# Weight conversion and weight product moved eight units earlier, reloaded weights split at a lower rate

## The chip, the cores and the metric

The kernel runs on one core of a Trainium2 chip. The metric is the device time of one execution in microseconds (us); of the kernel before there are three runs with a median of 712.68 us (711.45 to 714.77). The engines are named as the profile names them: PE is TensorE (PEld its weight loads), DVE is VectorE, ACT is ScalarE, POOL is GpSimd, and SP is the engine that issues nearly all DMAs, in order.

## The reference

Three layers follow one another. The first is attention over 2 x 8 heads, 768 rows and 64 columns per head, where a row sees only keys of the same hash bucket (six bits, the signs of a small projection). The second takes the attention's output x (1536 x 512) and multiplies it with four weights. The third routes each row to one of eight experts.

```python
h = (x @ w1) * (x @ w2) @ w3          # w1, w2: 512 x 1024, w3: 1024 x 1024
y = h @ w_out                         # w_out: 1024 x 512
e = argmax(y @ w_gate + modality_bias[modality_id])
out[mask] = gate_w[mask, None] * (relu(y[mask] @ e_w1[e]) @ e_w2[e])   # per expert e
```

The weights w1, w2, w3 and w_out arrive as 64-bit floats. In the kernel every operand of the second and third layer is split in a high and a low part, and each product is made of three matmuls (high-high, high-low, low-high).

## The kernel before, in words

**Units.** The attention part is one loop over i (L719). Unit i has a first stage (L312): two matmuls make the scores `m` of 128 query rows of one head, and DVE takes their row maximum (L324). There are 96 such units: pair of heads i // 12, and in it row block and head. The second stage (L345) follows nine units later: four matmuls make transposed scores `s`, ACT takes the exponential `pt` (L353), POOL adds it up in `acc` (L359; one in six on DVE near the end). Two units later still, two times two matmuls multiply `pt` with v (`a`, L367). Every six units PE transposes the row maxima (`f`, L335), for which four small POOL instructions (L328 to L331) have to be done first, and every twelve units it sums `acc` (`n`, L383).

**Weights.** Beside this the loop converts the weights, in 40 pieces of 128 x 512. A piece is loaded by SP into a ring of three buffers `cr` (L439), three DVE instructions turn its 64-bit patterns into 32-bit floats (L484, L485, L474), and then a piece of w_out or w3 is split: ACT copies the high part (L465), POOL subtracts (L466). A piece of w1 or w2 is written to a DRAM tensor `wfd` instead (L480), since there is no room for it yet. How many pieces are begun by the end of unit i is a ramp through points (unit, pieces), `RAMP` (L36): none by unit 7, 10 by unit 19, all by unit 84. The DVE instructions of a piece are popped from a list at three places of each unit (`fill`, L489).

**The product.** w3 times w_out is folded to one matrix: 8 x 8 x 3 = 192 matmuls of 128 x 128 by 512 (L544), `W34_STEP` = 3.1 per unit, taken from a list in `w34_step` (L556) as soon as both halves of the w3 row block are split. Each eighth is evacuated, written to DRAM and multiplied with the gate weights by three small PE steps in the units behind it (`wt` L519, `pg` L527, `pt` L535).

**Reload.** At unit `SWITCH` = 86 the buffers of the conversion are given back (L721), the tiles `w12` for w1 and w2 take their room, and the 16 pieces of `wfd` are loaded (`st`, L442) and split: ACT copies (L465), DVE subtracts (L466). They are begun at `RATE2` = 1.4 per unit, counted from unit 87 on (L844). At units 90 to 95 the first 256 rows of the attention's output are normalised (`norm_step`, L589): two DVE instructions (L581, L583) with one of POOL between them (L582), an ACT copy (L585) and a DVE subtraction (L587). From unit 95 to 104 a unit has no `m` any more, or one last, and takes twelve matmuls of the next layer (L618) in its place.

**What sets the order.** All of this is one list per engine, written in the order of the Python code; each engine runs its own list in order and waits where an operand or buffer isn't ready. So an instruction that waits holds up everything behind it on its engine.

Of the kernel before, what the change touches and what calls it, by code (L numbers as in the profile page):

```python
# [21 lines left out]
HP = H // 2  # L22
# [10 lines left out]
NCH = NT // CH  # L33

PRE = 0
RAMP = ((7, 0), (19, 10), (84, 41))  # L36
RATE2 = 1.4
W34_STEP = 3.1
SWITCH = 86
LEAD = 9  # L40
NDVE = 0
ACC_DVE = ((76, ()), (96, (2,)))
# [12 lines left out]
NSTEP = 4  # L55
# [36 lines left out]
def pieces_at(i):  # L92
    for (a, x), (b, y) in zip(RAMP, RAMP[1:]):
        if i < b:
            return int(x + (y - x) * max(i - a, 0) / (b - a))
    return RAMP[-1][1]

# [59 lines left out]
def body(tc, qT, kT, vP, w1d, w2d, w3d, wod, mod, wgate, mbias, e1, e2, cst, out):  # L157
# [30 lines left out]
    def ps(tag, shape, name):  # L188
        return psum[0].tile(shape, F32, tag=tag, name=name, bufs=nbuf.get(tag, 1))
# [220 lines left out]
    r_wo = ring("wo", 2 * 8 * DM, 1)  # L410
    wo = r_wo([P, 2, 8, DM], F32R)
    w3_t, raws, w12 = {}, {}, {}
    order = list(range(8))
    w3i, w12i = list(range(8, 24)), list(range(24, 40))
    while w3i or w12i:
        for k in PATTERN:
            src = w3i if k else w12i
# [3 lines left out]
    done = {"n": 0, "w": 0, "q": 0}  # L421
    dq, misc = [], []

    def piece_load(k):
        i = order[k]
        if k in raws:
            return
        if i < 8:
            src = wod[i * P:(i + 1) * P, :]
        elif i < 24:  # L430
            f, hf = divmod(i - 8, 2)
            src = w3d[f, :, hf * 4:hf * 4 + 4, :].rearrange("p g f -> p (g f)")
        else:
            m, j = divmod((i - 24) % 16, 8)
            c, hf = divmod(j, 2)
            src = ((w1d, w2d)[m] if i < 40 else wfd[m])[c * P:(c + 1) * P, hf * 512:hf * 512 + 512]
        if i < 40:
            raws[k] = r_cr([P, 1024])
            SP.dma_start(raws[k].bitcast(I64), src)  # L439
        else:  # L440
            raws[k] = r_st([P, 512])
            SP.dma_start(raws[k], src)  # L442
# [64 lines left out]
    w34q = []  # L507
# [5 lines left out]
    def after(n, fn):  # L513
        todo_at.setdefault(slot[0] + n, []).append(fn)

    def w34_t(f, ev):
        t = ps("m", [P, 4, P], f"wt{f}")
        for c in range(4):
            PE.transpose(t[:, c, :], ev[:, c * P:c * P + P], ident)  # L519
        wT = r_wT([P, 4, P])  # L520
        ACT.copy(wT, t)
        after(1, lambda: w34_gate(f, wT))
# [17 lines left out]
    def w34_mm(f, g, k):  # L540
        if g == 0 and k == 0:
            w34p[f] = ps("w", [P, DM], f"w{f}")
        st, mv = ((0, 0), (0, 1), (1, 0))[k]
        PE.matmul(w34p[f], w3_t[f][:, st, g, :], wo[:, mv, g, :], start=(g == 0 and k == 0), stop=(g == 7 and k == 2))  # L544
        if g == 7 and k == 2:
            ev = r_ev([P, DM])
            ACT.copy(ev, w34p.pop(f))
            SP.dma_start(w34d[f * P:(f + 1) * P, :], ev)
            after(1, lambda: w34_t(f, ev))

    for f in range(8):
        for g in range(8):
            for k in range(3):
                w34q.append((f, lambda f=f, g=g, k=k: w34_mm(f, g, k)))

    def w34_step(n):  # L556
        while n and done["w"] < len(w34q) and order.index(9 + 2 * w34q[done["w"]][0]) < done["n"]:
            w34q[done["w"]][1]()
            done["w"] += 1
            n -= 1  # L560
            if done["w"] % 24 == 0:
                break
# [26 lines left out]
    def norm_step(ch, step):  # L589
        for hp, part in ((step - 2, 2), (step - 1, 1), (step, 0)):  # L590
            if 0 <= hp < HP:
                norm_x(ch, hp, part)
# [126 lines left out]
    for i in range(NU + LEAD + LAG + 2):  # L719
        slot[0] = i  # L720
        if i == SWITCH:  # L721
            assert done["n"] == 40 and done["w"] == len(w34q), done
            for r in (r_cr, r_T, r_ev, r_wT, r_w3, r_wo):
                r.close()
            w12 = [one(f"w{m}", [P, 2, 4, DF], F32R) for m in range(2)]
            r_st = ring("st", 512, 3)
            for m in (40, 41, 42):
                piece_load(m)
            for r in (r_raw, r_bt, r_lo):
                r.close()  # L730
            rg["x"] = ring("x", 2 * HP * CH, 1, True)
            rg["rb"] = ring("rb", HP * CH, 1, True)
            rg["nw"] = ring("nw", CH, 1, True)
            rg["gf"] = ring("gf", 4 * CH, 1, True)
            rg["asb"] = ring("asb", CH, 1, True)
# [9 lines left out]
        if i == 12:  # L745
            SP.dma_start(cs[:, 160:], cst[:, 160:])
            SP.dma_start(wgs[:, :, 0:E], wgate.rearrange("(c p) e -> p c e", p=P))
        if i == SWITCH + NSTEP - 2:
            load_r(0)
        if 0 <= i - SWITCH - NSTEP < HP + 2:  # L750
            norm_step(0, i - SWITCH - NSTEP)
        if i == 98:
            load_r(1)
        if 101 <= i < 101 + HP:
# [22 lines left out]
        for fn in todo_at.pop(i, []):  # L777
            fn()
        w34_step(int((i + 1) * W34_STEP) - int(i * W34_STEP) if i < SWITCH - 1 else 1000)
        j = i - LEAD  # L780
# [10 lines left out]
        n = j - LAG - 1  # L791
# [46 lines left out]
        flush()  # L838
        if i < SWITCH - 1:
            want_pieces(min(40, pieces_at(i)))  # L840
        elif i < SWITCH + 2:
            want_pieces(40)
        else:
            want_pieces(min(56, 40 + int((i - SWITCH - 1) * RATE2)))  # L844
        if i == SWITCH - 1 or i >= NU + LEAD:
# [87 lines left out]
    for ch in range(NCH):  # L933
        if ch:
            g_t[ch] = rg["g"]([P, 2, 8, CH], F32R)
        for f in range(NEARLY if ch == 0 else 0, 8):
            if ch == 0:
                k = f - NEARLY
# [508 lines left out]
```

## Time and profile before

| | |
|---|---|
| median of three runs | 712.68 us |
| the profiled execution's own time | 713.29 us |
| its span, first to last instruction | 711.5 us |
| busy share: PE, DVE, ACT, POOL | 94%, 54%, 44%, 45% |
| attention part, until the last `m` | 0 to 300.5 us |
| mean granted clock of PE | 0.974 |

The profile is of one execution. Busy time of an engine is the time in which an instruction of it runs; a matmul's end is modelled, so where PE is busy all the time the step from start to start says more than the length. In a timeline several instructions of one kind that follow one another stand in one row with their count. The granted clock is a share of full speed: 1.0 is 2.4 GHz, 0.5 is 1.2 GHz. The chain of work that ended last is of no use here: the profile could follow it back for under a microsecond.

### The profile page before, as it was taken

What the parts mean: (1) busy time and instruction counts of PE and PEld (TensorE: products, weight loads), DVE (VectorE), ACT (ScalarE), POOL (GpSimd) and SP (SyncE); (2) the same over time, 40 slices, a digit from 0 to 9 for tenths busy, and PEclk for the clock granted to TensorE, in tenths of its full rate; (3) what the DMA queues carried; (4) which work ended last, traced back from release to release, by engine and by line L of the source; (5) the groups of instructions that cost most, each with busy time, mean ns of one, the idle gap of its engine ahead of it and who ended that gap; (6) DMA issues with size and microseconds to landing.
All of it is one profiled execution on the core that took longest, in us unless ns stands there. A gap on an engine that the chain in (4) does not pass through costs nothing. (4 is left out here: it accounts for less than half of the span.)

```text
span 711.5 us, 11037 instructions
## 1 busy us (share of the span) xinstructions
PE 666.1 (94%) x4004; PEld 506.4 (71%) x4004; DVE 382.2 (54%) x611; ACT 315.1 (44%) x534; POOL 320.6 (45%) x316
## 2 busy tenths in 40 slices
PE   5988999989998999799999999999998999999994
PEld 1444655656555655366999999898987999899983
DVE  6787675746576664857361212121175765665550
ACT  7255554535546554454341313131213765565551
POOL 8489767677767667555260505050214132011110
PEclk9599999999999999899999999999999999999998
DMA  7746545273645634230312020200017786766630
GB/s 226 238 169 171 199 136 182 78 210 103 194 140 144 198 99 128 88 120 1 107 48 60 2 59 1 60 1 30 1 53 270 269 286 232 235 207 210 209 119 5
DMA packets 42122, 94.06 MB, mean 132 GB/s; under 512 B 6784, under 2 KB 12464, under 8 KB 42064
## 3 DMA queue, kind: packets, MB, share of 16 engines
q1 hardware_dynamic: 39984, 86.76, 38.7%
q0 software_dynamic: 2080, 6.56, 2.7%
q8 instruction: 33, 0.54, 0.3%
q14 instruction: 25, 0.20, 0.1%
HBM read 72.98 MB, written 12.98 MB: 121 GB/s over the span
## 5 line engine op out<-in xcount | busy, mean ns | idle before, releaser
L618 PEld LDWEIGHTS ab<-x,w 128*128 128x128 f32 x1152 | 139.9, 191 | 10.5 <-issue 4.8
L618 PE MATMUL ab<-x,w 128*128 128x256 f32 x1152 | 144.5, 285 | 0.6 <-ACT ss L387 0.6
L324 DVE TENSOR_REDUCE nm<-m 128x1 f32<-128x768 f32 x96 | 91.1, 955 | 81.1 <-PE m L317 80.7
L359 POOL TENSOR_TENSOR acc<-acc,pt 128x770 f32<-128x770 f32 x61 | 113.4, 1860 | 31.6 <-ACT pt L353 30.7
L353 ACT ACTIVATE pt<-s 128x768 f32<-128x768 f32 x96 | 77.9, 812 | 104.8 <-PE s L352 91.7
L352 PE MATMUL s<-q,k 128*128 128x384 f32 (+1 forms) x384 | 88.1, 353 | 6.8 <-DVE nm L324 6.1
L629 POOL TENSOR_TENSOR g<-gf,g 128x256 fp32r<-128x256 f32 x48 | 35.4, 736 | 127.4 <-ACT g L628 127.2
L367 PE MATMUL a<-pt,v 128*64 128x385 f32 x384 | 86.3, 530 | 0.0
L352 PEld LDWEIGHTS s<-q,k 128*128 128x128 f32 (+1 forms) x384 | 71.1, 197 | 16.6 <-DVE nm L324 7.4
L1118 DVE TENSOR_TENSOR eu<-er,eu 128x1024 fp32r<-128x1024 f32 x56 | 67.4, 1223 | 23.0 <-ACT eu L1117 22.4
L317 PEld LDWEIGHTS m<-k,q 78*128 78x128 f32 x192 | 30.4, 198 | 64.7 <-issue 23.0
L1278 PE MATMUL e1F<-ex,eu 128*128 128x256 f32 x576 | 70.3, 284 | 0.5 <-DVE ex L1244 0.3
L1278 PEld LDWEIGHTS e1F<-ex,eu 128*128 128x128 f32 x576 | 69.7, 190 | 1.4 <-DVE ex L1244 0.5
L1304 POOL DMA_INDIRECT out<-o,sidx x13 | 13.6, 1045 | 124.7 <-ACT o L1303 119.8
L1296 PE MATMUL e2F<-eu,h 128*128 128x512 f32 x288 | 68.8, 395 | 0.0
L627 DVE TENSOR_TENSOR gf<-asb,ab 128x256 f32<-128x256 f32 x48 | 20.2, 421 | 90.4 <-ACT asb L626 90.3
L317 PE MATMUL m<-k,q 78*128 78x384 f32 x192 | 61.7, 405 | 5.7 <-DVE nm L324 2.3
L1296 PEld LDWEIGHTS e2F<-eu,h 128*128 128x128 f32 x288 | 53.4, 188 | 11.1
L1117 ACT CAST eu<-er 128x1024 fp32r<-128x1024 f32 x56 | 57.5, 1046 | 6.7 <-DMA er<-e 6.6
L544 PE MATMUL w<-wo,w 128*128 128x512 f32 x192 | 58.6, 413 | 0.8 <-POOL w L466 0.8
L914 PE MATMUL x2p<-w,g 128*128 128x512 f32 x240 | 58.1, 397 | 0.0
L359 POOL TENSOR_TENSOR acc<-pt,pt 128x770 f32<-128x770 f32 x16 | 29.6, 1851 | 52.4 <-ACT pt L353 52.4
(198 smaller groups left out, 780.6 us busy)
## 6 DMA issues: line engine op xcount, KB each, us to landing
er<-e SPq DMA_DIRECT2D x56, 512.0 KB
cr<-w3d SPq DMA_DIRECT2D x16, 512.0 KB
cr<-wod SPq DMA_DIRECT2D x8, 512.0 KB
cr<-w1d SPq DMA_DIRECT2D x8, 512.0 KB
wfd<-cT SPq DMA_DIRECT2D x16, 256.0 KB
cr<-w2d SPq DMA_DIRECT2D x8, 512.0 KB
st<-wfd SPq DMA_DIRECT2D x16, 256.0 KB
raw<-kT SPq DMA_DIRECT2D x8, 384.0 KB
```

Source lines behind the costliest of these rows:

```text
L317: PE.matmul(s[:, half, 0:HS], q[0:KROWS[hd], 0, qt * P:qt * P + P], k[0:KROWS[hd], 0, half * HS:half * HS + HS], start=True, stop=True,)
L324: DVE.tensor_reduce(nm[:, 3 * hd + qt % 3:3 * hd + qt % 3 + 1], s[:, :, 0:HS], AX.XY, ALU.max, negate=True)
L352: PE.matmul(s[:, hd, 0:HS], k[0:n, i, c * P:c * P + P], q[0:n, i, cl], start=(i == 0), stop=(i == 1))
L353: ACT.activation(pts[j % 4][:, :, 0:HS], s[:, :, 0:HS], AF.Exp, scale=SCALE)
L359: (DVE if on_dve else POOL).tensor_add(acc, pts[(j - 1) % 4] if c == 1 else acc, pts[j % 4])
L367: PE.matmul(a_t[p, half][64 * hd:64 * hd + 64, :], v[:, c, 64 * hd:64 * hd + 64], pts[j % 4][:, hd, :], start=(c == 0), stop=(c == QT - 1) ...
L544: PE.matmul(w34p[f], w3_t[f][:, st, g, :], wo[:, mv, g, :], start=(g == 0 and k == 0), stop=(g == 7 and k == 2))
L618: PE.matmul(ab[:, j, :], w12[j][:, st, c, fs], x[:, mv, c, :], start=(c == 0 and i == 0), stop=(c == 3 and i == 2))
L914: PE.matmul(st["ps"], g_t[ch][:, a, f, i * P:i * P + P], w34[b][:, f, :], start=(f == 0 and k == 0), stop=(f == 7 and k == 2),)
L1118: DVE.tensor_sub(t[:, 1, sl], raw, t[:, 0, sl].bitcast(F32))
L1278: PE.matmul(o[f], w[:, st, c, fs], x[:, mv, c, :], start=(c == 0 and i == 0), stop=(c == 3 and i == 2))
L1296: PE.matmul(o, h[:, st, f, sl], w[:, mv, f, :], start=(f == 0 and k == 0), stop=(f == 7 and k == 2))
```

## The change

It has four parts. The pieces come in another order: one half of the first w3 row block, four pieces of w_out, the other half, the other four, and then as before. `w34_step` asks for the two pieces that a matmul reads, with one piece between (until all 40 are split), where it asked for both halves of w3 before, so that the product can begin at unit 12. The ramp is steeper: 10 pieces by unit 17 and 40 by unit 76. The product has 2.95 matmuls per unit, and ends at unit 77. The conversion's buffers are given back at unit 78, and the reloaded pieces are begun at 0.8 per unit, counted from unit 79 on. What needs the room of the attention's raw inputs stays at unit 86 under the name `FREE`, and so do the normalisation and its load.

```diff
--- before.py
+++ after.py
@@ -33,10 +33,11 @@
 NCH = NT // CH
 
 PRE = 0
-RAMP = ((7, 0), (19, 10), (84, 41))
-RATE2 = 1.4
-W34_STEP = 3.1
-SWITCH = 86
+RAMP = ((7, 0), (17, 10), (76, 41))
+RATE2 = 0.8
+W34_STEP = 2.95
+SWITCH = 78
+FREE = 86
 LEAD = 9
 NDVE = 0
 ACC_DVE = ((76, ()), (96, (2,)))
@@ -410,8 +411,8 @@
     r_wo = ring("wo", 2 * 8 * DM, 1)
     wo = r_wo([P, 2, 8, DM], F32R)
     w3_t, raws, w12 = {}, {}, {}
-    order = list(range(8))
-    w3i, w12i = list(range(8, 24)), list(range(24, 40))
+    order = [8, 0, 1, 2, 3, 9, 4, 5, 6, 7]
+    w3i, w12i = list(range(10, 24)), list(range(24, 40))
     while w3i or w12i:
         for k in PATTERN:
             src = w3i if k else w12i
@@ -551,10 +552,10 @@
     for f in range(8):
         for g in range(8):
             for k in range(3):
-                w34q.append((f, lambda f=f, g=g, k=k: w34_mm(f, g, k)))
+                w34q.append(((g, 8 + 2 * f + g // 4), lambda f=f, g=g, k=k: w34_mm(f, g, k)))
 
     def w34_step(n):
-        while n and done["w"] < len(w34q) and order.index(9 + 2 * w34q[done["w"]][0]) < done["n"]:
+        while n and done["w"] < len(w34q) and max(map(order.index, w34q[done["w"]][0])) < done["n"] - 1 + (done["n"] == 40):
             w34q[done["w"]][1]()
             done["w"] += 1
             n -= 1
@@ -726,6 +727,7 @@
             r_st = ring("st", 512, 3)
             for m in (40, 41, 42):
                 piece_load(m)
+        if i == FREE:
             for r in (r_raw, r_bt, r_lo):
                 r.close()
             rg["x"] = ring("x", 2 * HP * CH, 1, True)
@@ -745,10 +747,10 @@
         if i == 12:
             SP.dma_start(cs[:, 160:], cst[:, 160:])
             SP.dma_start(wgs[:, :, 0:E], wgate.rearrange("(c p) e -> p c e", p=P))
-        if i == SWITCH + NSTEP - 2:
+        if i == FREE + NSTEP - 2:
             load_r(0)
-        if 0 <= i - SWITCH - NSTEP < HP + 2:
-            norm_step(0, i - SWITCH - NSTEP)
+        if 0 <= i - FREE - NSTEP < HP + 2:
+            norm_step(0, i - FREE - NSTEP)
         if i == 98:
             load_r(1)
         if 101 <= i < 101 + HP:
```

The list of PE at units 12 and 13, of the kernel before (`m_0_0` and `m_0_1` are the scores of units 12 and 13, `s` the transposed scores, `a` the product with v):

```order
L317 MATMUL m_0_0_308<-k_18_87,q_16_85 128x384 x2
L335 MATMUL f_1_316<-ident_70,nm_212 12x128
L352 MATMUL s_0_3_324<-q_12_81,k_14_83 128x384 x2
L352 MATMUL s_0_3_324<-q_13_82,k_15_84 128x384 x2
L367 MATMUL a_0_298<-pt_21_90,v_152 64x385 x2
L317 MATMUL m_0_1_339<-k_19_88,q_17_86 128x384 x2
L352 MATMUL s_0_4_346<-q_12_81,k_14_83 128x384 x2
L352 MATMUL s_0_4_346<-q_13_82,k_15_84 128x384 x2
```

and of the changed kernel:

```order
L318 MATMUL m_0_0_318<-k_18_87,q_16_85 128x384 x2
L336 MATMUL f_1_326<-ident_70,nm_212 12x128
L545 MATMUL w_332<-wo_93,w_43_252 128x512 x3
L353 MATMUL s_0_3_338<-q_12_81,k_14_83 128x384 x2
L353 MATMUL s_0_3_338<-q_13_82,k_15_84 128x384 x2
L368 MATMUL a_0_308<-pt_21_90,v_152 64x385 x2
L318 MATMUL m_0_1_353<-k_19_88,q_17_86 128x384 x2
L545 MATMUL w_332<-wo_93,w_43_252 128x512 x3
L353 MATMUL s_0_4_363<-q_12_81,k_14_83 128x384 x2
L353 MATMUL s_0_4_363<-q_13_82,k_15_84 128x384 x2
```

The first three matmuls of the product (`w`) stand in unit 12 now, the next three in unit 13; before, the first stood in unit 22. Between units 12 and 21 there are eight such groups of three.

The list of PE at units 78 and 79 (`m_3_0` and `m_3_1`), of the kernel before:

```order
L317 MATMUL m_3_0_2152<-k_14_83,q_12_81 128x384 x2
L335 MATMUL f_0_2157<-ident_70,nm_2001 12x128
L519 MATMUL wt_2163<-ident_70,ev_2132 128x128 x4
L544 MATMUL w_2170<-wo_93,w_181_1918 128x512 x3
L352 MATMUL s_1_3_2174<-q_16_85,k_18_87 128x384 x2
L352 MATMUL s_1_3_2174<-q_17_86,k_19_88 128x384 x2
L367 MATMUL a_1_2143<-pt_23_92,v_1660 64x385 x2
L317 MATMUL m_3_1_2185<-k_15_84,q_13_82 128x384 x2
L527 MATMUL pg_2190<-wT_2168,wgs_75 32x128 x4
```

and of the changed kernel:

```order
L318 MATMUL m_3_0_2222<-k_14_83,q_12_81 128x384 x2
L336 MATMUL f_0_2227<-ident_70,nm_2048 12x128
L520 MATMUL wt_2233<-ident_70,ev_2199 128x128 x4
L353 MATMUL s_1_3_2240<-q_16_85,k_18_87 128x384 x2
L353 MATMUL s_1_3_2240<-q_17_86,k_19_88 128x384 x2
L368 MATMUL a_1_2209<-pt_23_92,v_1715 64x385 x2
L318 MATMUL m_3_1_2251<-k_15_84,q_13_82 128x384 x2
```

The product's matmuls are gone from units 78 to 85, 24 in all. In unit 77 twelve stand together in place of three. The three small steps behind the last eighth (`wt`, `pg`, `pt`) came in units 86 to 88 and come in units 78 to 80 now.

The list of DVE from the row maximum of unit 91 (`m_3_1`) to that of unit 93 (`m_4_1`), of the kernel before; `w` from `st` is the subtraction of a reloaded piece:

```order
L324 TENSOR_REDUCE nm_2464<-m_3_1_2491 128x1
L466 TENSOR_TENSOR w_215_2368<-st_2374,w_215_2368 128x512
L466 TENSOR_TENSOR w_216_2369<-st_2455,w_216_2369 128x512
L587 TENSOR_TENSOR x_2485<-xT_10_79,x_2485 128x256
L581 TENSOR_SCALAR nw_2514<-rb_2414,mv_73 128x256
L583 TENSOR_TENSOR xT_10_79<-xT_10_79,nw_2514 128x256
L324 TENSOR_REDUCE nm_2464<-m_4_0_2518 128x1
L466 TENSOR_TENSOR w_215_2368<-st_2483,w_215_2368 128x512
L587 TENSOR_TENSOR x_2485<-xT_10_79,x_2485 128x256
L581 TENSOR_SCALAR nw_2537<-rb_2414,mv_73 128x256
L583 TENSOR_TENSOR xT_10_79<-xT_10_79,nw_2537 128x256
L324 TENSOR_REDUCE nm_2464<-m_4_1_2542 128x1
```

and of the changed kernel:

```order
L325 TENSOR_REDUCE nm_2488<-m_3_1_2515 128x1
L588 TENSOR_TENSOR x_2509<-xT_10_79,x_2509 128x256
L582 TENSOR_SCALAR nw_2530<-rb_2437,mv_73 128x256
L584 TENSOR_TENSOR xT_10_79<-xT_10_79,nw_2530 128x256
L325 TENSOR_REDUCE nm_2488<-m_4_0_2534 128x1
L467 TENSOR_TENSOR w_208_2214<-st_2457,w_208_2214 128x512
L588 TENSOR_TENSOR x_2509<-xT_10_79,x_2509 128x256
L582 TENSOR_SCALAR nw_2553<-rb_2437,mv_73 128x256
L584 TENSOR_TENSOR xT_10_79<-xT_10_79,nw_2553 128x256
L325 TENSOR_REDUCE nm_2488<-m_4_1_2558 128x1
```

Of the three subtractions of reloaded pieces one is left here. From the maximum of unit 90 to that of unit 94 there were six, and there are three. The others went to units 82 to 89.

## Rows read from the trace of the kernel before

**Rows 1.** Windows: stretch, busy us of PE PEld DVE ACT POOL, clock, DMA share, GB/s

```profile
24.40:35.10 10.70, 9.96 (x28) 5.41 (x27) 8.83 (x12) 4.74 (x7) 6.94 (x9) 0.55 0.59 176
35.10:60.40 25.30, 21.90 (x109) 11.08 (x107) 22.89 (x32) 14.80 (x23) 22.76 (x18) 0.99 0.47 154
60.40:243.70 183.30, 173.03 (x888) 104.27 (x888) 115.88 (x158) 97.16 (x147) 131.14 (x112) 0.99 0.53 160
243.70:269.50 25.80, 24.44 (x129) 14.84 (x127) 15.74 (x21) 13.24 (x21) 16.88 (x15) 1.00 0.42 123
269.50:278.80 9.30, 9.30 (x55) 5.39 (x53) 3.93 (x5) 4.51 (x8) 6.07 (x4) 1.00 0.66 180
278.80:299.90 21.10, 14.40 (x54) 7.52 (x52) 18.26 (x24) 9.63 (x19) 11.52 (x13) 0.84 0.24 81
```

**Rows 2.** Windows, line L544 (the product of weights) alone, two of these stretches

```profile
60.40:243.70 183.30, 51.35 (x168) 29.75 (x168) 0.99 0.53 160
243.70:269.50 25.80, 7.25 (x24) 4.17 (x24) 1.00 0.42 123
```

**Rows 3.** Timeline, PE: start us, us, line, operation, count; full clock

```profile
96.93 0.86 PE L544 MATMUL w<-wo,w 128*128 128x512 f32 x3
97.63 0.86 PE L352 MATMUL s<-q,k 78*128 78x384 f32 x4
...
276.80 0.62 PE L317 MATMUL m<-k,q 128*128 128x384 f32 x2
...
278.84 0.62 PE L317 MATMUL m<-k,q 78*128 78x384 f32 x2
```

**Rows 4.** Timeline, PE: a triple of L544 at the half clock

```profile
148.21 1.47 PE L544 MATMUL w<-wo,w 128*128 128x512 f32 x3
149.48 1.48 PE L352 MATMUL s<-q,k 78*128 78x384 f32 x4
```

**Rows 5.** Groups by line, DVE, 24.4 to 60.4 us: count, busy us, mean ns, idle before

```profile
L324 DVE TENSOR_REDUCE nm<-m 128x1 f32<-128x768 f32 x12 | 11.4, 953 | 3.3 <-PE m L317 3.3
L485 DVE SCALAR_TENSOR_TENSOR u<-cr,u 128x512 int32<-128x512 int32 x10 | 6.9, 694 | 0.3
L484 DVE TENSOR_SCALAR u<-cr 128x512 int32<-128x512 int32 x10 | 6.9, 686 | 0.1
L474 DVE SCALAR_TENSOR_TENSOR cT<-cr,u 128x512 int32<-128x512 int32 x9 | 6.2, 686 | 0.7
```

**Rows 6.** Groups by line, POOL, 24.4 to 60.4 us

```profile
L359 POOL TENSOR_TENSOR acc<-acc,pt 128x770 f32<-128x770 f32 x8 | 14.6, 1829 | 0.1
L466 POOL TENSOR_TENSOR wo<-cT,wo 128x512 fp32r<-128x512 f32 x8 | 11.0, 1374 | 0.1
```

**Rows 7.** Waits of PE, 60.4 to 243.7 us: us in total, times, longest us

```profile
PE f L335 <- POOL nm L331: 5.5, 5, 1.5
...
PE w L544 <- POOL w L466: 0.8, 1, 0.8
```

**Rows 8.** Waits of PE, 243.7 to 300 us

```profile
PE s L352 <- DVE nm L324: 4.6, 2, 3.9
PE f L335 <- POOL nm L331: 1.6, 1, 1.6
```

**Rows 9.** Timeline, DVE, 281 to 299 us

```profile
283.85 1.92 DVE L466 TENSOR_TENSOR w<-st,w 128x512 fp32r<-128x512 f32 x1 [0.81 <-ACT w L465]
...
287.81 2.50 DVE L466 TENSOR_TENSOR w<-st,w 128x512 fp32r<-128x512 f32 x2
290.23 2.03 DVE L587 TENSOR_TENSOR x<-xT,x 128x256 fp32r<-128x256 f32 x1
...
294.22 0.68 DVE L466 TENSOR_TENSOR w<-st,w 128x512 fp32r<-128x512 f32 x1
```

**Rows 10.** Groups by line, DVE, 278.8 to 299.9 us

```profile
L466 DVE TENSOR_TENSOR w<-st,w 128x512 fp32r<-128x512 f32 x7 | 7.1, 1032 | 0.8 <-ACT w L465 0.8
```

**Rows 11.** Timeline, POOL, 281 to 294 us

```profile
283.39 1.82 POOL L359 TENSOR_TENSOR acc<-acc,pt 128x770 f32<-128x770 f32 x1 [1.68 <-ACT pt L353]
```

## The prediction

> **What bounds the kernel now.** I read the busy shares first: PE has 94%, the others about half. The change touches only the attention part, so I cut that by windows at the starts of units, then asked for PE's waits in each, and read the timelines where PE waits. The reader is to see five stretches of different kind in [rows 1].
>
> Units 10 to 21 (24.4 to 60.4 us) are not PE's. From 35.1 us on DVE is busy 22.89 of 25.30 us and POOL 22.76. A unit with a piece costs DVE one row maximum and three conversions, 0.953 + 0.686 + 0.694 + 0.686 = 3.02 us [rows 5]; PE needs less. Before 35.1 us PE's granted clock is 0.55, the lower of its two levels (1.2 GHz) for most of that time, and the 3.3 us in which DVE waited for the scores `m` [rows 5] lie largely there.
>
> Units 22 to 77 (to 243.7 us) and 78 to 85 (to 269.5) are PE's: 173.03 of 183.30 and 24.44 of 25.80 us busy. Units 86 to 89 are PE's too, 9.30 of 9.30 us, but cheap: a unit without the product takes 278.84 - 276.80 = 2.04 us [rows 3]. The product costs three matmuls in 97.63 - 96.93 = 0.70 us, 0.233 each [rows 3]. Units 90 to 94 are DVE's: 21.10 us in which PE has 14.40 busy and DVE 18.26, at a clock of 0.84 [rows 1]; PE waits there 4.6 us for row maxima, 3.9 of them at once [rows 8]. Units 95 to 104 the change leaves as they are.
>
> **The change part by part.**
>
> *Units 9 to 22.* By the ramp 12 pieces are converted through unit 22 where there were 10: two more pieces, 2 x 2.07 = 4.13 us of DVE, on the engine that sets the pace. Beside them PE gets eight triples of the product, which fit: 2.04 + 0.70 is under 3.02. At the half clock they don't: a triple takes 149.48 - 148.21 = 1.27 us there [rows 4], and the first two, in units 12 and 13, may stand before the clock rises. Bounds: the best case hides the two pieces in DVE's 3.3 us of waiting, +0.8 us; the worst hides nothing and adds both slow triples, 4.13 + 2.54 = +6.7. About half of the waiting should remain, because PE sets the pace there at its lower clock, so 4.13 - 1.65, and half of one slow triple, 0.6: I take **+3.0**.
>
> *Units 22 to 77.* The product has 168 matmuls in this stretch before [rows 2], 3 of them in unit 22; after, 192 - 24 = 168 in units 23 to 77. Three more: **+0.7**. The conversion's pieces are 28 for 27, beside a PE that DVE (115.88 of 183.30 us) and POOL (131.14) follow easily; nothing for them. Should that cover be gone, a piece costs at most its 2.07 us.
>
> *Units 78 to 85.* The 24 matmuls of the product [rows 2] go, on an engine that was busy throughout: 24 x 0.233 = **-5.6**. What is late next is POOL. Its 16.88 us [rows 1] stay while the stretch shrinks to 25.8 - 5.6 = 20.2, which is 84% busy, and PE's `f` in units 78 and 84 waits for four POOL instructions behind an accumulation. Where it waited for them it lost 5.5 us in five times, at most 1.5 [rows 7], and 1.6 us once behind this stretch [rows 8]. Bounds for two of them: 0 to +3.2; one average wait is nearest, **+1.1**. The steps `wt`, `pg`, `pt` only move along, from a stretch of PE's to another one. SP's first three reloads stand in front of the moves of the last pair's hash bits now; those are wanted six units later, so that costs nothing unless SP is held for over 12 us.
>
> *Units 86 to 94.* Three reloaded pieces fewer between the row maxima of units 90 and 94, and DVE sets the pace there. One subtraction took 1.032 us in the mean [rows 10]; alone it took 0.68, and 1.92 at worst [rows 9]. Bounds -2.0 and -5.8; I take the mean, **-3.1**. The upper end is unlikely, since POOL stands right behind DVE there: an accumulation of 1.82 us [rows 11] and a multiplication in most units.
>
> Why one instruction has such different lengths: the subtraction began at 283.85 while POOL's accumulation of 283.39 ran until 285.21, and ended 0.56 us after it [rows 9, 11], as if it had stood still. The Trainium skill says the same (SBUF — State Buffer, "Who interferes with whom"): a DVE instruction with two SBUF inputs and a GpSimd instruction that reads SBUF exclude each other, and the second to start is held until the first is done. The trace agrees, with the 0.56 us. The rule speaks against part of this change: the subtractions that move to units 82 to 89 have two SBUF inputs as well, and POOL accumulates in most of these units.
>
> *Sum.* 3.0 + 0.7 - 5.6 + 1.1 - 3.1 = -3.9 us. The profiled execution took 713.29 us (span 711.5, and 1.8 around it), so 709.4; the median of the runs lies 0.6 lower, at 712.68, so **708.8 us**. No change can be told within 0.5%, that is 709.1 to 716.2.
>
> **The rivals.**
>
> *Slower: the early product waits for POOL's splits.* Each early triple reads a piece whose low part POOL has written one or two units before. With a piece in every unit POOL has 1.83 us of accumulation in five units of six and 1.374 us of split [rows 6], 2.9 of 3.02 us; if it falls behind by one accumulation, PE stands at the triple, and with it all scores behind it. For it: the one triple that came right behind its split waited 0.8 us [rows 7]. Against it: there is a whole piece between. Price: eight triples; 0.28 us of a wait is hidden in each DVE-paced unit (3.02 less 2.04 + 0.70). From 1.2 us a wait on, 8 x 0.92 = 7.4 eats the gain and 0.5% more; at 1.6 us it is 10.6, thus 719.
>
> *No difference: the moved subtractions give the gain back.* In units 82 to 89 seven or eight of them meet POOL's accumulations. If each one holds either engine for the 1.24 us by which 1.92 exceeds 0.68 [rows 9], DVE and POOL have some 9 us more, the row maxima and `f` come later, and units 78 to 89 keep most of their old length: -5.6 + 1.1 becomes about -1. That gives 713.29 + 3.0 + 0.7 - 1.0 - 3.1, less 0.6: 712.3. For it: POOL's share in the stretch rises to 84%. Against it: DVE is busy for 15.74 of 25.80 us there and 3.93 of 9.30 in the four units behind [rows 1], so it has room for them.
>
> *More is gained.* The early pieces hide (+0.8) and the jam in units 91 to 93 goes wholly, with both long subtractions and the 2.03 us one of the normalisation that was held like them [rows 9]: -5.8. Then 0.8 + 0.7 - 5.6 + 1.1 - 5.8 = -8.8, or 703.9. For it: the clock of 0.84 says that PE's own work was slower there too, and that would mend with it.
>
> *The change doesn't do what it says.* The lists show that it does; this has no chance of its own.
>
> **How the numbers follow.** My forecast has 0.42, and from the terms' bounds its own range is 706 to 711.5; three fifths of that lie below 709.1. More gained 0.20, no difference 0.25, slower 0.13. Faster by over 0.5%: 0.25 + 0.20 = 0.45 and a little of the no-difference case, 0.47. Slower: 0.12, since a mild case of that rival stays within 0.5%. The rest, 0.41, is no difference that can be measured. The range that leaves out 2 in 10 reaches from the case of more gain to past the case of none, 704 to 715.
>
> **What would show it.** In the changed kernel's timeline of PE the score `m` of unit 22 should start about 3 us later than now (60.4 us), that of unit 78 about 3.7 later than 243.7, that of unit 86 about 1 earlier than 269.5, and that of unit 95 about 4 earlier than 299.9; from there on all runs in step. DVE should show no wait for `m` of note between 36 and 58 us, and the windows of units 78 to 85 no product. I am wrong early if PE waits for POOL's splits at the product between units 12 and 21, or if unit 22 starts no later than before; wrong late if units 78 to 89 shrink by less than 3 us, or if a wait of PE for row maxima of over 3 us stays in units 90 to 94.

## The result and the profile after

The changed kernel takes **718.88 us** (median of four runs, 718.33 to 719.61); the kernel before took 712.46 beside it. The ratio is 1.0083, with a 95% interval of 1.0064 to 1.0103: it is slower by 0.83%, or 5.9 us, and the forecast of 708.8 was wrong in sign. The profiled execution took 719.09 us, its span is 717.3 (before 711.5).

The stretches between the same units as in [rows 1], of the changed kernel (windows; busy us of PE, PEld, DVE, ACT, POOL, granted clock, DMA share, GB/s):

```profile
24.54:36.30 11.76, 9.38 (x37) 5.18 (x37) 11.07 (x16) 5.68 (x9) 8.80 (x10) 0.85 0.69 205
36.30:61.50 25.20, 24.95 (x125) 13.67 (x123) 23.85 (x33) 14.80 (x23) 23.71 (x19) 1.00 0.54 177
61.50:253.20 191.70, 176.58 (x903) 106.79 (x901) 118.58 (x163) 97.90 (x149) 129.58 (x111) 0.97 0.52 157
253.20:277.80 24.60, 21.75 (x106) 11.82 (x104) 11.33 (x13) 14.77 (x24) 18.53 (x14) 0.86 0.44 131
277.80:287.20 9.40, 8.64 (x43) 4.73 (x41) 6.68 (x6) 4.93 (x9) 5.34 (x3) 1.00 0.29 85
287.20:306.30 19.10, 13.67 (x51) 6.74 (x51) 16.76 (x23) 7.77 (x14) 11.48 (x12) 0.87 0.28 80
```

The units' starts by the timeline of PE (`m`) give this table; a difference is the changed kernel's length of the stretch less that of the kernel before:

| units | before, us | after, us | difference | forecast |
|---|---|---|---|---|
| to the start of 22 | 60.41 | 61.48 | +1.1 | +3.0 |
| 22 to 77 | 183.29 | 191.72 | **+8.4** | +0.7 |
| 78 to 85 | 25.84 | 24.56 | **-1.3** | -4.5 |
| 86 to 94 | 30.32 | 28.57 | -1.8 | -3.1 |
| from 95 on | 411.6 | 411.0 | -0.7 | 0 |

The clock fell from 0.99 to 0.97 in units 22 to 77 and from 1.00 to 0.86 in units 78 to 85. The waits of PE (us in total, times, longest) show why. In units 22 to 77, against [rows 7]:

```profile
PE f L336 <- POOL nm L332: 8.8, 5, 2.9
PE wt L520 <- DVE bt L250: 1.5, 1, 1.5
PE pt L536 <- DVE bt L250: 1.4, 1, 1.4
PE pg L528 <- ACT rT L338: 1.0, 1, 1.0
PE pg L528 <- DVE bt L250: 0.9, 1, 0.9
```

and in units 78 to 94, against [rows 8]:

```profile
PE f L336 <- POOL nm L332: 4.9, 2, 2.5
PE s L353 <- DVE nm L325: 2.7, 4, 1.3
```

PE waited 5.5 us for `f` before and waits 8.8 now; the small steps behind the product (`wt`, `pg`, `pt`) cost it 4.9 us, where such waits of over 0.5 us were 2.8 before. In units 78 to 94 the row maxima cost less than before (2.7 for 4.6 us), but `f` more: 4.9 us for 2.4, since the kernel before has one more wait there, in unit 84, beside the 1.6 us of [rows 8] (waits of PE, 243.7 to 300 us):

```profile
PE f L335 <- ACT q L269: 0.8, 1, 0.8
```

The waits at `f` have two shapes. In unit 60 (timelines of POOL, then PE: start, length; in brackets the idle time before and its releaser):

```profile
183.56 1.82 POOL L285 TENSOR_TENSOR k<-raw,k 64x768 fp32r<-64x768 f32 x1
185.35 1.26 POOL L467 TENSOR_TENSOR w<-cT,w 128x512 fp32r<-128x512 f32 x1
186.59 0.22 POOL L329 TENSOR_SCALAR nm<-nm 128x6 f32<-128x6 f32 x1
```

```profile
187.69 0.28 PE L336 MATMUL f<-ident,nm 128*12 128x128 f32 x1 [2.06 <-POOL nm L332]
...
189.26 1.55 PE L368 MATMUL a<-pt,v 128*64 128x385 f32 x4
```

The kernel before has the same place on POOL without the split of a w3 piece:

```profile
183.69 1.81 POOL L284 TENSOR_TENSOR k<-raw,k 64x768 fp32r<-64x768 f32 x1
185.49 0.22 POOL L328 TENSOR_SCALAR nm<-nm 128x6 f32<-128x6 f32 x1
```

So a split (L467, 1.26 us) of a piece that the ramp has moved here stands in front of the four small instructions, behind an accumulation and the split of k (L285, 1.82 us). `f` waits 2.06 us, where it waited 0.58 before. After it PE is at its lower level: `a` takes 1.55 us where it took 0.87. In unit 72 it is another cause (DVE, POOL, PE):

```profile
228.23 0.69 DVE L485 TENSOR_SCALAR u<-cr 128x512 int32<-128x512 int32 x1 [3.46 <-DMA cr<-w2d]
228.96 0.70 DVE L486 SCALAR_TENSOR_TENSOR u<-cr,u 128x512 int32<-128x512 int32 x1
229.56 0.95 DVE L325 TENSOR_REDUCE nm<-m 128x1 f32<-128x768 f32 x1
```

```profile
226.47 1.81 POOL L285 TENSOR_TENSOR k<-raw,k 64x768 fp32r<-64x768 f32 x1
230.60 0.23 POOL L329 TENSOR_SCALAR nm<-nm 128x6 f32<-128x6 f32 x1 [2.32 <-DVE nm L325]
```

```profile
231.71 0.28 PE L336 MATMUL f<-ident,nm 128*12 128x128 f32 x1 [2.92 <-POOL nm L332]
```

DVE stands 3.46 us at a conversion whose load has not come, the row maximum that `f` needs stands behind that conversion, and POOL, long ready, waits for the maximum. In the 4 us after each of these two waits the granted clock was 0.64 and 0.69, a mix of the two levels (windows, PE alone):

```profile
187.60:191.60 4.00, 3.91 (x14) 0.64 0.61 219
231.60:235.60 4.00, 3.89 (x14) 0.69 0.95 320
```

### The profile page after: what moved, and what is told of

It is laid out like the page before. It is cut to its first block, busy times and chain, and to the rows that moved or that the text cites. A ratio compares the mean times of both kernels' runs of the same rounds, so it can differ in the third digit from the quotient of the medians.

```text
span 717.3 us, 11027 instructions
## 1 busy us (share of the span) xinstructions
PE 667.1 (93%) x4004; PEld 506.1 (71%) x4004; DVE 382.5 (53%) x611; ACT 315.4 (44%) x534; POOL 321.4 (45%) x316
## 5 line engine op out<-in xcount | busy, mean ns | idle before, releaser
L619 PEld LDWEIGHTS ab<-x,w 128*128 128x128 f32 x1152 | 139.9, 191 | 10.5 <-issue 4.4
L545 PE MATMUL w<-wo,w 128*128 128x512 f32 x192 | 59.3, 416 | 0.1
L916 PEld LDWEIGHTS x2p<-w,g 128*128 128x128 f32 x240 | 44.2, 188 | 11.4 <-issue 2.1
```

What stands on the lines that cost most here:

```text
L619: PE.matmul(ab[:, j, :], w12[j][:, st, c, fs], x[:, mv, c, :], start=(c == 0 and i == 0), stop=(c == 3 and i == 2))
L916: PE.matmul(st["ps"], g_t[ch][:, a, f, i * P:i * P + P], w34[b][:, f, :], start=(f == 0 and k == 0), stop=(f == 7 and k == 2),)
```

## The experiments

All comparisons are ratios to the kernel before on the same chip, with 95% intervals. 0.1% is 0.7 us.

**The parts alone.** Two kernels undo parts of the change. The first keeps only the new order of pieces and the two-piece condition of the product (the edit, in one line).

```diff
-RAMP = ((7, 0), (17, 10), (76, 41)); RATE2 = 0.8; W34_STEP = 2.95; SWITCH = 78
+RAMP = ((7, 0), (19, 10), (84, 41)); RATE2 = 1.4; W34_STEP = 3.1; SWITCH = 86
```

> The kernel before with the first two parts of the change alone: the new order of pieces and the product that follows two pieces; ramp, 3.1 matmuls per unit, unit 86 and 1.4 as before. The product begins at unit 13 and ends at unit 81. Theory (bunching): little is bunched (units 58 to 60 and 66, 67), the early matmuls lie beside DVE, so 24 of them are saved, 5.6 us, less 1 to 2 us of delay: 707.5 to 710. Rival (moved subtractions): the reload is as before, so likewise 707.5 to 710. A rival that blames the early product itself: not below the kernel before, 712 to 717.

Measured: 710.09 us, 0.9966 [0.9950, 0.9982], a hair above what was expected. This part gains 2.4 us. The second puts only the reload back (`RATE2 = 1.4`, `SWITCH = 86`).

> The changed kernel with the buffers given back at unit 86 and the reload at 1.4 per unit, as before; the conversion is as dense as in the changed kernel, and the product ends at unit 81. Theory (POOL's chain in front of f): the loss between units 60 and 77 stays, the wait at unit 84 too, since PE has no product there either, and the jam of units 90 to 94 returns: 717 to 721. Rival (moved subtractions): they are back where they were, so the loss at units 84 to 90 goes and more: 713 to 716.

Measured: 716.13 us, 1.0040 [1.0017, 1.0063], just above the rival's range and below the theory's. So the three parts are worth, in this order: new order and early product -0.34%; steeper ramp with 2.95 matmuls per unit +0.74%; moved reload +0.43%. The part that was to give 3.1 us costs as much. Its price holds one thing more: with `SWITCH` back at 86 the product runs to unit 81 again, with nine of its matmuls in units 78 to 81 that stand in unit 77 in the changed kernel.

**Bunching and loads.** After the change eight pieces in a row stand in units 65 to 72. One kernel spreads the pieces evenly (`order` filled from a list of ones and zeros that never lets the room for w3 hold a piece up):

> The changed kernel with another order of the pieces and nothing else: no piece of w3 is due before the product has freed its buffer, so pieces come every second unit from unit 20 to 76 instead of eight in a row in units 65 to 72. The product's list is the same. Theory (bunching: eight pieces in a row make DVE the pace, outrun the loads, and let PE fall to its lower clock): most of the 7.8 us that the changed kernel lost between units 60 and 77 return, 711 to 713.5 us. Rival (the subtractions moved to units 82 to 89 block POOL's port): the place of the loss is untouched, 718 to 719.5.

Measured: 722.41 us, 1.0124 [1.0085, 1.0162], above both ranges. DVE waits for no load in its profile, yet `f` waits 2.04 us in unit 60, 2.02 in 72 and 2.02 in 36, and a split stands in front of it in all three. The spread trades late loads for splits in front of `f`, so it does not tell what the bunch costs. The kernel before with a bunch (`PATTERN = (1, 1, 1, 1, 0)`):

> The kernel before with the pattern of the order changed from three w3 to two w1/w2 pieces into four to one, and nothing else: now fifteen pieces come in a row, one per unit, from unit 70 to 84. The product's list stays as it was within one or two matmuls. Theory (bunching): 5 to 12 us slower than the kernel before, 717.5 to 724.5, with DVE waiting for loads. Rival (moved subtractions) and rival (early product): none of either is in it, 712 to 713.5.

Measured: 716.72 us, 1.0063 [1.0043, 1.0083]: a bunch costs something, under what was expected, and in the profile DVE waits 1.78 and 2.33 us for loads in units 83 and 84. Four load buffers for three, each load issued one piece earlier, on the changed kernel:

> The changed kernel with four load buffers for the pieces in place of three, each load issued one piece earlier. If the bunch hurts because loads land late (DVE waited 4.9 us for them, PE's f 2.9 us behind that, then the half clock): 3 to 5 us back, 714 to 716. If it hurts by DVE's work alone: 717.5 to 719. The rival of the moved subtractions: 718 to 719.5.

Measured: 718.36 us, 1.0080 [1.0053, 1.0107]. DVE's waits for loads are gone and `f` in unit 72 waits 0.58 us, yet the times show no gain. In the profile units 22 to 77 did become shorter, 187.8 us for 191.7; but the profiled execution of the changed kernel had come to unit 22 3.6 us earlier, at a clock of 0.88 for 0.60 until 36 us. By itself the time said that the loads don't matter; that was wrong, as shown below.

**POOL's chain at f.** The first of the two splits of k goes one unit ahead, away from `f`:

```diff
             if ph in (10, 11):
                 q_hi(p + 1, ph - 10, 1)
-                k_lo(p + 1, ph - 10)
+            if ph in (9, 11):
+                k_lo(p + 1, (ph - 9) // 2)
```

On the changed kernel:

> The changed kernel with one edit: POOL's first low-part subtraction of k for the next pair (1.82 us) stands one unit earlier, so that it no longer lies in front of the four small instructions that PE's f waits for every twelve units. New theory (POOL's chain in front of f): the change took PE's work away from in front of f or put a split there, the waits for f grew from 7.9 to 13.7 us between 24 and 308 us, most of them over 2 us, and PE fell to its lower clock behind four of them. Then the waits of units 24 to 84 fall below 1 us each, the half clock behind units 60, 72 and 84 goes, and 7 to 11 us return: 707.5 to 712. Rival (subtractions moved to units 82 to 89 block POOL's port): only the wait at unit 84 shrinks, 716 to 718.5.

Measured: 713.29 us, 0.9998 [0.9979, 1.0016], a little short of the expected range. On the kernel before:

> The kernel before with the same single edit. Theory (POOL's chain in front of f): its six waits there were 0.6 to 1.5 us with one fall of the clock, so 4 to 6 us are gained: 706.5 to 709. If the waits have another cause: 712 to 713.5.

Measured: 706.54 us, 0.9911 [0.9884, 0.9938]. On the kernel with the new order and early product alone:

> The kernel with the new order and the early product alone (710.1 us) and the same edit. Theory (POOL's chain): its waits for f at units 24, 48, 60, 72, 84 were 0.8 to 2.1 us, 4 to 5 us are gained: 705 to 707. If the waits have another cause: 709.5 to 711.

Measured: **702.98 us, 0.9856 [0.9836, 0.9876]**, better than expected. This one beats both kernels, by 10.4 us (713.41 beside it) and 15.9 us (718.88).

The edit is worth much the same on all: 0.85% on the changed kernel, 0.89% before, 1.1% on the last. So POOL's chain is a price that every version pays and **not what makes the changed kernel the slower one**. What is left in its trace says where to look: one wait of PE for `f` of 3.3 us before unit 78, in unit 72 (waits, PE):

```profile
PE f L336 <- POOL nm L332: 3.6, 2, 3.3
```

and DVE there, in the same kernel, behind a late load (timeline):

```profile
223.97 0.69 DVE L485 TENSOR_SCALAR u<-cr 128x512 int32<-128x512 int32 x1 [3.85 <-DMA cr<-w2d]
224.69 0.70 DVE L486 SCALAR_TENSOR_TENSOR u<-cr,u 128x512 int32<-128x512 int32 x1
225.30 0.95 DVE L325 TENSOR_REDUCE nm<-m 128x1 f32<-128x768 f32 x1
```

**Both causes.** The earlier split of k and four buffers together, on the changed kernel:

> The changed kernel with two edits together: the split of k one unit earlier (713.29 by itself) and four buffers for the loads of the conversion, each issued one piece earlier (718.36 by itself). In the trace with the earlier split one long wait of PE for f is left before unit 78, 3.31 us in unit 72, and there POOL's four small instructions wait for a row maximum of DVE that stands behind a conversion whose load was late by 3.85 us. Theory: two causes stand behind one another at f, POOL's chain and the loads, and each hides when only the other is mended. Then this goes to 709 to 712, with no wait for loads and no wait for f over 1 us between units 60 and 78. Rival: the loads are without effect here as they were by themselves: 713 to 714.5.

Measured: 708.01 us, 0.9927 [0.9900, 0.9954]. The row of PE's waits for `f` over the same units is down to

```profile
PE f L336 <- POOL nm L332: 0.3, 1, 0.3
```

The control, the kernel before with both:

> A control: the kernel before with the earlier split of k (ratio 0.9911) and four load buffers. In its trace DVE does not wait for a load once. Theory: only the steeper ramp outruns the loads, so the fourth buffer does nothing here: ratio 0.989 to 0.993 (705 to 708). Rival: the fourth buffer helps every kernel of this kind, and the gain from 0.9998 to 0.9927 says nothing about the ramp: 0.984 to 0.987 (701.5 to 704).

Measured: 705.69 us, 0.9890 [0.9862, 0.9918], as without the buffer (0.9911). The fourth buffer takes 0.71% from the changed kernel and nothing that can be told (0.21%) from the kernel before, in whose profile DVE never waited for a load. So the late loads belong to the change, by the profiles above all, since the two effects differ by no more than their joint interval of 0.5%. Without the earlier split the buffer took 0.03% from the changed kernel, with it 0.71%, and this difference is clear of noise (0.7%, give or take 0.5). That the loads hid behind POOL's chain is argued from it, and not shown at one place: with the loads alone mended, `f` waited 0.58 us in unit 72, and still 1.25 to 2.52 us in units 24, 48, 60, 84 and 90.

**The moved reload.** The changed kernel with the earlier split of k, reload as before:

> The changed kernel with the split of k one unit earlier and the reload as before (from unit 86, 1.4 per unit); the steeper ramp, the new order and 2.95 matmuls per unit stay. Without the earlier split the old reload was worth 2.75 us (716.13 for 718.88). Theory: most of that was the wait for f in unit 84, in which the split of k stood beside the moved subtractions; with the split elsewhere the reload's place matters little, and this is within 1 us of the 713.29 with the moved reload: 712.3 to 714.3. Rival: the moved subtractions cost by themselves, wherever the split stands: 709.5 to 711.5. Either way what is left to the 702.98 of the kernel with the old ramp is the price of the steeper ramp.

Measured: 709.49 us (705.27 to 713.98), 0.9943 [0.9920, 0.9966]: the rival was right, the moved reload costs 0.55% here too. With four buffers as well:

> The changed kernel with the earlier split of k, four load buffers, and the reload as before (unit 86, 1.4 per unit). Of the change only the new order, the steeper ramp and 2.95 matmuls per unit are left. Theory: the moved reload costs 3 to 4 us by itself, as it did with three buffers (a ratio of 1.0083 against 1.0040, and 0.9998 against 0.9943), since its subtractions lengthen the waits for f in units 84 and 90 in every run that has them; then the ratio to the kernel before falls from 0.9927 to 0.987 to 0.9895 (703.5 to 705.5 at a median of 713 before), near the 0.9856 of the kernel with the old ramp. Rival: that difference was the loads again, whose wait in unit 72 varies from execution to execution; then the ratio stays at 0.991 to 0.9945 (706.5 to 709).

Measured: 704.74 us, 0.9886 [0.9856, 0.9915], against 0.9927: 0.41%. Each of the last two intervals reaches into the other, but three pairs of kernels agree on 0.4 to 0.55%. Their profiles show the place. With the moved reload (waits of PE from 230 us on)

```profile
PE f L336 <- POOL nm L332: 3.9, 2, 2.6
PE s L353 <- DVE nm L325: 3.1, 4, 1.3
```

and with the old one

```profile
PE s L353 <- DVE nm L325: 4.1, 2, 3.1
PE f L336 <- POOL nm L332: 2.4, 2, 1.6
```

The gain at the row maxima is there (4.1 down to 3.1 us), and `f` takes more than that back (2.4 up to 3.9, and 0.7 more in unit 95 that is put down to ACT). From unit 84 to 92 the moved reload is slower by 4.3 us, and from there to 95 faster by 2.7. At unit 90 it looks so, in the kernel with the moved reload (DVE, POOL, PE):

```profile
274.51 1.53 DVE L468 TENSOR_TENSOR w<-st,w 128x512 fp32r<-128x512 f32 x1 [0.90 <-ACT w L467]
275.96 0.94 DVE L325 TENSOR_REDUCE nm<-m 128x1 f32<-128x768 f32 x1
276.82 0.95 DVE L360 TENSOR_TENSOR acc<-acc,pt 128x770 f32<-128x770 f32 x1
```

```profile
273.62 1.87 POOL L360 TENSOR_TENSOR acc<-pt,pt 128x770 f32<-128x770 f32 x1 [1.43 <-ACT pt L354]
276.99 0.87 POOL L329 TENSOR_SCALAR nm<-nm 128x6 f32<-128x6 f32 x1 [1.50 <-DVE nm L325]
277.94 0.48 POOL L330 TENSOR_TENSOR nm<-nm 128x6 f32<-128x6 f32 x1
```

```profile
279.09 0.28 PE L336 MATMUL f<-ident,nm 128*12 128x128 f32 x1 [2.60 <-POOL nm L332]
```

The subtraction of a reloaded piece stands in front of the row maximum that `f` needs. It waits 0.90 us for ACT's copy of the high part; then POOL's accumulation of 273.62 begins first, and the subtraction takes 1.53 us and ends 0.55 us after it, as one did before [rows 9, 11]. The maximum comes at 275.96, POOL starts 1.50 us late, and its first small instruction meets DVE's accumulation of 276.82 and takes 0.87 us, where 0.22 is usual. PE waits 2.60 us for `f`.

Does the holding cost, or the place? In the next pair the subtraction is an instruction with one SBUF input, so that it waits for no copy of ACT either (the kernels of this pair and the next leave out the low parts of w1 and w2):

```diff
-            (POOL if NDVE <= k < 40 else DVE).tensor_sub(lo, T, hi.bitcast(F32))
+            if k < 40: POOL.tensor_sub(lo, T, hi.bitcast(F32))
+            else:      DVE.tensor_scalar(lo, T, 0.5, None, ALU.mult)
```

> The changed kernel with the earlier split of k and four load buffers (ratio 0.9927), in which the DVE instruction of a reloaded piece has one SBUF input in place of two: it multiplies the piece by one half, where it subtracted the high part from it. The low parts of w1 and w2 are not computed by this; count, place and size of the instructions stay. Theory: the moved subtractions cost time because they and POOL's instructions hold each other. Then none of the 16 takes over 0.8 us (mean now 1.183), POOL's four small instructions in front of f in unit 90 are not held, that wait of f falls from 2.60 us to 1.7 or less, and the ratio falls to 0.986 to 0.990. Rival: what costs is where they stand in DVE's list, between the row maxima; then the waits and the ratio stay, 0.991 to 0.995.

> The same edit on the kernel with the reload as before (ratio 0.9886); again the low parts of w1 and w2 are not computed. Theory: here the held instructions stand in units 90 to 95, where DVE sets the pace (mean 1.045 us of each), and the wait of 3.12 us for row maxima in unit 92 goes or falls under 1.5: ratio 0.984 to 0.987. If holding costs only in units 78 to 90, that is with the moved reload: no change, 0.987 to 0.990.

Measured: 705.59 us, 0.9893 [0.9866, 0.9919] with the moved reload, 703.06 us, 0.9852 [0.9829, 0.9874] with the old one. Both fall by 0.34%, into the ranges that were expected if the holding costs, and the move stays 0.41% dearer. With the moved reload `f` waits no more in unit 84 and less in unit 90 (waits of PE from 230 us on):

```profile
PE f L336 <- POOL nm L332: 1.1, 1, 1.1
```

With the old one the wait of 3.12 us for row maxima is still 2.87. But the edit did not do what it was to do: the multiplication takes 0.41 us where it runs alone or begins first, and one still took 2.02 us beside POOL's accumulations (DVE, then POOL, with the moved reload):

```profile
266.31 2.02 DVE L471 TENSOR_SCALAR w<-st 128x512 fp32r<-128x512 f32 x1
...
269.11 0.41 DVE L471 TENSOR_SCALAR w<-st 128x512 fp32r<-128x512 f32 x1
```

```profile
262.31 5.73 POOL L360 TENSOR_TENSOR acc<-acc,pt 128x770 f32<-128x770 f32 x3
```

So a third pair keeps the length and takes away the holding: `DVE.tensor_reduce(lo, T.rearrange("p (n o) -> p n o", o=1), AX.X, ALU.max)` in place of the multiplication.

> The instruction with one SBUF input of the last pair of kernels was quicker alone (0.41 us for the subtraction's 0.68) and was still held beside POOL (2.02 us at worst), so length and holding were not told apart. Here the subtraction of a reloaded piece becomes a maximum over rows of one element: one SBUF input, one element per step as the row maxima, which in no trace were longer than 0.96 us beside POOL. The low parts of w1 and w2 are not computed. Moved reload, earlier split of k, four buffers (with the subtraction 0.9927). If it is the holding that costs: each of the 16 takes 0.6 to 0.75 us, the wait for f in unit 90 falls from 2.60 to under 1.9, ratio 0.987 to 0.990. If it is place and length: 0.991 to 0.994.

> The same edit with the reload as before (with the subtraction 0.9886). If the holding costs in either place: 0.984 to 0.987, and the moved reload stays 0.3 to 0.5% behind. If holding is what makes the move dear, the two kernels come within 0.15% of each other.

Measured: 701.41 us, **0.9850** [0.9830, 0.9870] with the moved reload, better than expected, and 703.14 us, 0.9873 [0.9854, 0.9892] with the old one. In the kernel with the moved reload (groups, DVE: count, busy us, mean ns; waits of PE, both from 230 us on)

```profile
L471 DVE TENSOR_REDUCE w<-st 128x512 fp32r<-128x512 f32 x13 | 8.8, 677 | 0.0
```

```profile
PE s L353 <- DVE nm L325: 4.0, 2, 3.0
PE f L336 <- POOL nm L332: 1.3, 1, 1.3
```

the 13 such instructions in this window take 0.67 or 0.68 us each, in unit 84 PE does not wait for `f`, and in unit 90 1.3 us for 2.60. The move is no longer dearer: it is 0.23% ahead, in intervals that overlap, where it was 0.41% behind. So by these pairs neither the place nor the length is what makes the moved reload dear: the place is the same, and 0.68 us is the length of a subtraction that nothing holds.

What is left is the holding and the wait for ACT's copy, and both pairs take away the second. The times speak for the holding: from the multiplication to the reduction, neither of which waits for ACT, the kernel with the moved reload gains 0.43%, though the instruction became longer by 0.27 us, and with the old reload the same exchange loses 0.21%. But the intervals of these pairs touch, and the profiles do not show the gain: the profiled executions of the two kernels with the moved reload took 704.74 and 704.82 us, and `f` waits in them nearly alike. And in unit 84 of the kernel with the subtraction (DVE, POOL, PE) the copy alone was late:

```profile
259.08 0.69 DVE L468 TENSOR_TENSOR w<-st,w 128x512 fp32r<-128x512 f32 x1 [2.44 <-ACT w L467]
```

```profile
260.73 0.23 POOL L329 TENSOR_SCALAR nm<-nm 128x6 f32<-128x6 f32 x1 [1.55 <-DVE nm L325]
```

```profile
261.82 0.28 PE L336 MATMUL f<-ident,nm 128*12 128x128 f32 x1 [1.30 <-POOL nm L332]
```

This subtraction took 0.69 us, so nothing held it. It waited 2.44 us for the copy, the maximum behind it came late, and POOL and PE waited for that. How the price of the move divides between the copy and the holding stays open; the copy by itself was not tried. With the old reload the time falls by 0.13% against the subtraction, which can't be told from nothing.

**A milder move.** The best kernel with reload from unit 84 at 1.1 per unit, and the ramp to 41 at unit 82:

> The best so far (702.98: new order and two-piece gate, old ramp, old reload, k split one unit earlier) with a mild form of the moved reload: ramp to 41 at unit 82, reload from unit 84 at 1.1 per unit. If the wait of 3.12 us for row maxima in unit 92 comes from reloaded pieces that crowd there, it goes: 700 to 702.5. If the crowding only moves: 702.5 to 704. If the steeper ramp's cost shows already at two units: 704 to 706.

Measured: 706.00 us, 0.9903 [0.9870, 0.9937], against 0.9856. `f` in unit 90 waits 2.5 us again (1.6 without the edit), and a wait of 3.1 us for row maxima stays. Even this much does not pay. Since the ramp moves too, by two units, the times do not tell which of the two costs; in the profile the difference lies in units 86 to 94 (30.5 us for 27.9).

## Why the prediction was wrong

*Units 9 to 22, +3.0.* The size holds. This execution shows +1.1, since its clock rose early (0.85 in its first window, where [rows 1] have 0.55); four other kernels, with the same lists up to unit 20, show from +2.9 to +3.5. The profile lists no wait of PE at the product there: the rival of late splits fell.

*Units 22 to 77, +0.7: the first step that failed.* "The conversion's pieces are 28 for 27, beside a PE that DVE and POOL follow easily; nothing for them." Busy shares of 63% and 72% said so. But `f` does not wait for a share. It waits for what stands in front of it in two lists at that moment, and the ramp changed that: a split in front of it in unit 60, a late load in front of its maximum in 72. In the profile `f` costs 3.3 us more and the small steps 2.1 (4.88 for 2.82, counting waits over 0.5 us). The product adds nothing, and the +0.7 was a miscount: of the 168 matmuls before, three stand in unit 22, but the whole stretch has 168 after too (windows, L545 alone, for [rows 2]):

```profile
61.48:253.20 191.72, 51.47 (x168) 0.97 0.52 157
```

What is left of the 8.4, 3.0 us, goes to the small steps of one more eighth, which ran in units 86 to 88 before, and to the lower clock behind the waits. By the runs the ramp and its step rate cost 0.74%, and 0.87% with the split of k out of the way; 0.57 of that, give or take 0.4, was the loads (0.9943 to 0.9886), and the other 0.3% can't be told from nothing.

*Units 78 to 85, -5.6 + 1.1: the second term was too small.* The matmuls went, 24 of them: up to unit 84 the stretch was shorter by 4.4 us, which is what the 19 that stood there had cost. The other five were worth 1.2, but units 84 and 85 together became 3.1 us longer: a wait of 2.33 us at `f` and half the clock. So the lateness cost 4.3 us in this execution, where 1.1 was set and 3.2 was the bound. In the profiles of the kernels with spread pieces and with four buffers, whose lists are the same here, it is 2.0 and 3.3. The prediction's own sign showed: units 78 to 89 shrank by 1.2 us, less than 3.

*Units 86 to 94, -3.1: the second step that failed.* The profile shows -1.8, but this says nothing of the reload: kernels that keep the old one, with the subtraction, show from +0.8 to -2.9 in the same units, and their longest wait for row maxima there is 2.5 to 3.9 us. By the runs the move costs 0.4 to 0.55%. The term counted what leaves units 90 to 94. What arrives in units 78 to 90 was left to a rival, "no difference", which saw that subtractions would meet POOL's accumulations and make `f` late; `f` did come late, but I had taken it for a draw at worst. And the rival priced only the holding, at some 9 us for seven or eight subtractions. The profile has six in units 83 to 89 (groups by line, DVE, 266 to 287.5 us: count, busy us, mean ns, idle before):

```profile
L467 DVE TENSOR_TENSOR w<-st,w 128x512 fp32r<-128x512 f32 x6 | 6.7, 1110 | 10.5 <-ACT w L466 10.5
```

Together they are 2.5 us longer than six of 0.69, and DVE stood 10.5 us in front of them for ACT's copies, which the prediction put at nothing without a reason. With neither holding nor that wait the move is ahead by 0.23%, 1.6 us (0.9873 to 0.9850), half of the term and within the noise. The subtractions that stay are no quicker either: five now take 1.252 us in the mean, for 1.032 [rows 10] (groups by line, DVE, 287.2 to 306.3 us; the first began in unit 89):

```profile
L467 DVE TENSOR_TENSOR w<-st,w 128x512 fp32r<-128x512 f32 x5 | 6.3, 1252 | 1.4 <-ACT w L466 1.4
```

The rule of the Trainium skill that was weighed (SBUF — State Buffer, "Who interferes with whom") spoke against this part, and was given the smaller chance. The last two pairs agree with the rest of that section too: it lets DVE's `tensor_scalar` enter a mode that takes the shared port with one input, and says that `tensor_reduce` never contends on this chip. The one was held for 2.02 us, the other never (all 16 in the trace at 0.67 to 0.68).

The forecast of the rest, no effect from unit 95 on, held within 0.7 us.

## What to carry to other kernels

Where an engine waits at one recurring place, write out what stands in front of that place in every list that feeds it, before and after the change; a low busy share of the feeding engine is no cover. A cause that shows no effect when it is mended alone may stand behind another: mend both, and put the same mend on the kernel before as a control. Of work that is moved, price the place where it arrives as carefully as the place that it leaves: what it will wait for there, and what will wait behind it.

## What the runs showed of the hardware

In the profile of the changed kernel the matmuls behind waits of PE of 2.06, 2.92, 2.33 and 2.54 us (units 60, 72, 84, 90) ran partly at the lower clock level, `a` in 1.55 for 0.87 us, so that there a wait cost more than its length. The length of the wait alone does not decide this: in the same profile the granted clock was 0.59 over the 4 us behind a wait of 1.26 us (unit 48) and 1.00 behind one of 1.74 (unit 24), and in that of the kernel with four buffers alone it was 1.00 behind one of 2.52 (unit 90). And one SBUF input is not enough to keep DVE clear of POOL: over 128 x 512 values a multiplication took 0.41 us alone and up to 2.02 beside POOL, a subtraction 0.68 and up to 1.92 [rows 9], a reduction over single elements always 0.68.
